# Retention and a feed-forward block on one core: written order on all engines, turns of q and k by DMA, one load list

## The chip, the cores and the metric

The kernel runs on one core of one Trainium2 chip. The metric is the device time of one execution in microseconds (us), given as the median of several. All medians, ratios and profiles below are of undisturbed ("fast") runs, except where one run is called slow. A ratio is the mean time of one kernel's fast runs over the mean of the other kernel's fast runs of the same rounds on the same chip, so it is not quite the ratio of the medians that are quoted. Intervals are 95%.

TensorE (PE in the profile) does the matrix products, VectorE (DVE), ScalarE (ACT) and GpSimd (POOL) the rest, and SyncE (SP) issues the transfers. SPq is its transfer queue.

## The reference

```python
# q, k, v: (8 batches, 8 heads, 576 tokens, 64), f32
scores = scale * q @ k.T                       # per batch and head
Dmat   = where(i >= j, gamma[h] ** (i - j), 0) # causal decay
x      = ((scores * Dmat) @ v)                 # then to (4608 tokens, 512)
out    = gelu_tanh(x @ w_in) @ w_out           # w_in 512x2048, w_out 2048x512
```

A batch is 576 tokens, that is four chunks of 128 and a tail of 64. Within a chunk the retention is computed from masked scores; what earlier chunks contribute goes through a running state (k^T v, scaled and added from chunk to chunk, the "scan"). The feed-forward part runs over nine blocks of 512 tokens. Each block has an up half (64 products `hp` with w_in, then a GELU into `gT`) and a down half (64 products `op` with w_out).

## The kernel before

The retention of batch b+1 is put between the feed-forward steps of block b. q and k come in as token rows and must be turned (transposed) before the scores. TensorE does that, and VectorE copies the result out of PSUM. Only TensorE follows the written order; a scheduler orders the other engines. All transfers go through one queue. The code here is shortened.

```python
def tr_pair(b, p):                       # turn four chunks of one head pair, one copy
    for i, key in enumerate("kq"):
        for c in range(NC):
            nc.tensor.transpose(t[:, 512*i + 128*c : ...], a[key][...], ident)
    nc.vector.tensor_copy(out=s, in_=t)  # "qk"

def att_steps(b):                        # ten pieces, all four chunks in each
    return [tr_pair 0, tr_pair 1, tr_tail, scores 0-1 + states + scan,
            tr_pair 2, tr_pair 3, scores 2 + tail, values 0-1, scores 3, values 2-3]

slots = {1: 0, 2: 1, 3: 2, 5: 3, 7: 4, 8: 5, 11: 6, 14: 7, 16: 8, 19: 9}
with tc.manual_schedule(engines={PE}):
    load_batch(0); cast_batch(0, ...)
    for g in range(4): load_w_in(g)
    load_batch(1)
    ...                                  # retention of batch 0, casts of w_in
    for f in range(NF): load_w_out(f)
    for f in range(NF): cast_w_out(f)
    for t in range(NTB):                 # feed-forward block t, with the pieces in its slots
        ...
```

Of the kernel before, what the change touches and what calls it, by code (L numbers as in the profile page):

```python
# [19 lines left out]
def kernel(  # L20
# [9 lines left out]







# [9 lines left out]
    NF = DF // 128  # L46
    scale = 1.0 / math.sqrt(D)
# [4 lines left out]
    ps = ctx.enter_context(tc.tile_pool(name="ps", bufs=2, space=PSUM))  # L52

    def bank(tag, bufs, name, dt=F32):
        return ps.tile([128, 512 if dt == F32 else 1024], dt, tag=tag, name=name, bufs=bufs)


    ident = const.tile([128, 128], F16, name="ident")
    make_identity(nc, ident)

    pos_i = const.tile([128, 1], I32, name="pos_i")
    nc.gpsimd.iota(pos_i, pattern=[[0, 1]], base=-64, channel_multiplier=1)
    pos = const.tile([128, 1], F32, name="pos")
    nc.vector.tensor_copy(out=pos, in_=pos_i)
    post = const.tile([128, 1], F32, name="post")
    nc.vector.tensor_copy(out=post[0:64], in_=pos[0:64])
    nc.vector.tensor_scalar(out=post[64:128], in0=pos[64:128], scalar1=-64.0, scalar2=None, op0=ALU.add)
    ex = const.tile([128, 24], F32, name="ex")
    for h in range(H):
        lg = math.log(gam[h])  # L70
        nc.vector.tensor_scalar(out=ex[:, h : h + 1], in0=pos, scalar1=lg, scalar2=None, op0=ALU.mult)
        nc.vector.tensor_scalar(out=ex[:, 8 + h : 9 + h], in0=pos, scalar1=-lg, scalar2=None, op0=ALU.mult)
        u, hh = divmod(h, 4)
        pr = slice(64 * u, 64 * u + 64)
        nc.vector.tensor_scalar(out=ex[pr, 16 + hh : 17 + hh], in0=post[pr], scalar1=lg, scalar2=None, op0=ALU.mult)
        nc.vector.tensor_scalar(out=ex[pr, 20 + hh : 21 + hh], in0=post[pr], scalar1=-lg, scalar2=None, op0=ALU.mult)
# [3 lines left out]
    nc.vector.tensor_scalar(out=sc[:, 16:20], in0=sc[:, 16:20], scalar1=scale, scalar2=None, op0=ALU.mult)  # L80

    gt = const.tile([128, HP, 64], F32, name="gt")
    for h in range(H):
        u = 64 * (h % 2)
        nc.gpsimd.memset(gt[u : u + 64, h // 2, :], gam[h] ** 128)

    cm = const.tile([128, NC, 128], F32, name="cm")
    nc.gpsimd.memset(cm, 1.0)
    nc.gpsimd.affine_select(
        out=cm, in_=cm, compare_op=ALU.is_ge, fill=0.0, base=0,  # L90
        pattern=[[0, NC], [1, 128]], channel_multiplier=-1,
    )
    tm = const.tile([128, 2, 128], F32, name="tm")
    nc.gpsimd.tensor_copy(out=tm, in_=cm[:, 0:2, :])
    nc.gpsimd.memset(tm[0:64, :, 64:128], 0.0)

    tbd = []
    for i in range(2):
        t = const.tile([128, NC, HP, 128], F16, name=f"tbd{i}")
        nc.gpsimd.memset(t, 0.0)  # L100
        tbd.append(t)

    w_in_sb = const.tile([128, 4, DF], F16, name="w_in_sb")
    w_out_sb = const.tile([128, NF, DM], F16, name="w_out_sb")
    xT = const.tile([128, HP, NT], F16, name="xT")


    def ld():
        return sb.tile([128, 512], F32, tag="ld", name="ld", bufs=15)

    att = {}

    def load_batch(b):
        att[b] = a = {"raw": {}}
        for c in range(NC):
            for key, src in (("k", k), ("q", q), ("v", v)):
                t = ld()
                nc.sync.dma_start(  # L118
                    out=t.rearrange("p (h d) -> p h d", d=D),
                    in_=src[b, :, 128 * c : 128 * c + 128, :].rearrange("h s d -> s h d"),  # L120
                )
                a["raw"][key, c] = t
        for key, src in (("k", k), ("q", q), ("v", v)):
            t = ld()
            for u in range(2):
                nc.sync.dma_start(
                    out=t[64 * u : 64 * u + 64, 0:256].rearrange("p (h d) -> p h d", d=D),
                    in_=src[b, 4 * u : 4 * u + 4, M0:S, :].rearrange("h s d -> s h d"),
                )
            a["raw"][key, NC] = t  # L130

    def cast_batch(b, eng):
        a = att[b]
        for key in "kqv":
            a[key] = sb.tile([128, NC * 512 + 256], F16, tag="c" + key, name="c" + key, bufs=2)
        for c in range(NC + 1):
            for key in "kqv":
                w = 512 if c < NC else 256
                raw = a["raw"][key, c][:, 0:w]
                dst = a[key][:, 512 * c : 512 * c + w]  # L140
                if key == "v":
                    eng[key].tensor_copy(out=dst, in_=raw)  # L142
                else:
                    s0 = {"q": 0, "k": 8}[key] if c < NC else {"q": 16, "k": 20}[key]
                    nh = w // D
                    eng[key].tensor_tensor(  # L146
                        out=dst.rearrange("p (h d) -> p h d", d=D),
                        in0=raw.rearrange("p (h d) -> p h d", d=D),
                        in1=sc[:, s0 : s0 + nh].unsqueeze(2).to_broadcast([128, nh, D]),
                        op=ALU.mult,  # L150
                    )
        del a["raw"]

    w_raw = {}

    def load_w_in(g):
        for ct in range(4):
            t = ld()
            nc.sync.dma_start(out=t, in_=moe_w_in[128 * ct : 128 * ct + 128, 512 * g : 512 * g + 512])
            w_raw["i", g, ct] = t  # L160

    def load_w_out(f):
        t = ld()
        nc.sync.dma_start(out=t, in_=moe_w_out[128 * f : 128 * f + 128, :])
        w_raw["o", f] = t

    def cast_w(n, dst, src):
        if n % 2 == 0:
            nc.vector.tensor_copy(out=dst, in_=src)
        else:  # L170
            nc.scalar.copy(out=dst, in_=src)  # L171

    def cast_w_in(g):
        for ct in range(4):
            cast_w(ct, w_in_sb[:, ct, 512 * g : 512 * g + 512], w_raw.pop(("i", g, ct)))

    def cast_w_out(f):
        cast_w(f, w_out_sb[:, f, :], w_raw.pop(("o", f)))

# [4 lines left out]
    def tr_pair(b, p):  # L184
        a = att[b]
        t = bank("att", 6, "tr", F16)
        for i, key in enumerate("kq"):
            for c in range(NC):
                nc.tensor.transpose(  # L189
                    t[:, 512 * i + 128 * c : 512 * i + 128 * c + 128],  # L190
                    a[key][:, 512 * c + 128 * p : 512 * c + 128 * p + 128],
                    ident,
                )
        s = sb.tile([128, 1024], F16, tag="qk", name="qk", bufs=6)
        nc.vector.tensor_copy(out=s, in_=t)  # L195
        a["qk", p] = s

    def tr_tail(b):
        a = att[b]
        t = bank("att", 6, "tr", F16)  # L200
        for i, key in enumerate("kq"):
            for s in range(2):
                nc.tensor.transpose(
                    t[:, 256 * i + 128 * s : 256 * i + 128 * s + 128],
                    a[key][:, 512 * NC + 128 * s : 512 * NC + 128 * s + 128],
                    ident,
                )
        s = sb.tile([128, 512], F16, tag="qkt", name="qkt", bufs=2)
        nc.vector.tensor_copy(out=s, in_=t[:, 0:512])
        a["qkt"] = s  # L210

    def score_pairs(b, pairs, tail):
        a = att[b]
        todo = []
        for p in pairs:
            st = [bank("att", 6, "st") for _ in range(2)]
            qk = a["qk", p]
            for c in range(NC):
                for hl in range(2):
                    r = slice(64 * hl, 64 * hl + 64)  # L220
                    nc.tensor.matmul(  # L221
                        st[hl][:, 128 * c : 128 * c + 128],
                        qk[r, 128 * c : 128 * c + 128],
                        qk[r, 512 + 128 * c : 512 + 128 * c + 128],
                        start=True, stop=True,
                    )
            for hl in range(2):
                todo.append((("ret", p, hl), st[hl], 512))
        if tail:
            st = [bank("att", 6, "st") for _ in range(2)]  # L230
            qk = a["qkt"]
            for s in range(2):
                for hl in range(2):
                    r = slice(64 * hl, 64 * hl + 64)
                    nc.tensor.matmul(
                        st[hl][:, 128 * s : 128 * s + 128],
                        qk[r, 128 * s : 128 * s + 128],
                        qk[r, 256 + 128 * s : 256 + 128 * s + 128],
                        start=True, stop=True,
                    )  # L240
            for hl in range(2):
                todo.append((("rett", hl), st[hl], 256))
# [145 lines left out]
    with tc.manual_schedule(engines={PE}):  # L388
        load_batch(0)
        cast_batch(0, {"k": nc.vector, "q": nc.gpsimd, "v": nc.gpsimd})  # L390
        for g in range(4):
            load_w_in(g)
# [51 lines left out]
```

## Time and profile before

Median 361.18 us (360.8 to 361.42 in three runs). The profiled span is 358.8 us.

| stretch of the trace | us |
|---|---|
| block 0 ends (start of the whole until then) | 87.06 |
| block 1 | 35.47 |
| block 2 | 35.13 |
| blocks 3 to 6 | 35.12, 35.93, 35.50, 35.50 |
| blocks 7 and 8 without retention, and the end | 59.09 |

The way to read such a kernel is to find the first `hp` of each block in TensorE's timeline and to take differences. TensorE is busy for nearly all of every block after block 0, so there its own work and its short waits set the time. In block 0 it is busy 53.21 of 87.06 us, so there something else does.

### The profile page before, as it was taken

Reading aid. Unit: us, or ns where it says so; the run is one execution under the profiler, and the core shown is the slowest. Engines: PE = TensorE matmul, PEld = TensorE weight load, DVE = VectorE, ACT = ScalarE, POOL = GpSimd, SP = SyncE. Lnnn points to the kernel's source line nnn. Section 1 sums busy time; section 2 is a strip of 40 time slices with the busy share of each in tenths; the row PEclk is TensorE's granted clock in tenths of the full one; section 3 lists DMA queues with packets and bytes.
Section 4 is the critical chain, followed back from the end, with each engine's and each line's share of the span. In section 5 each row is a group of like instructions: output and inputs, shape, how many; then the busy total and the mean of one; then the engine's idle time right before and its main releaser. Section 6 shows DMA issues by size and latency. Waiting matters only on the chain.

```text
span 358.8 us, 6008 instructions
## 1 busy us (share of the span) xinstructions
PE 316.4 (88%) x2400; PEld 159.1 (44%) x2400; DVE 125.9 (35%) x269; ACT 161.9 (45%) x303; POOL 70.3 (20%) x101
## 2 busy tenths in 40 slices
PE   0176368799999999999999999999999999999995
PEld 0153134344544454455445544554454444444442
DVE  5287238430762174227422771172117200000000
ACT  1037318722682268236723662366236624714721
POOL 8610430342051333232321232000000000000000
PEclk9995669899999999999999999999999999999999
DMA  9979989994692898598937931100110011011012
GB/s 173 205 230 319 224 193 360 219 188 134 144 218 81 194 225 163 127 235 170 194 108 187 216 82 58 58 2 2 58 60 0 2 60 58 0 60 59 0 38 79
DMA packets 122715, 46.52 MB, mean 130 GB/s; under 512 B 113984, under 2 KB 113984, under 8 KB 122688
## 3 DMA queue, kind: packets, MB, share of 16 engines
q1 hardware_dynamic: 122688, 46.15, 55.2%
q8 instruction: 18, 0.29, 0.4%
q14 instruction: 9, 0.07, 0.1%
HBM read 36.70 MB, written 9.44 MB: 129 GB/s over the span
## 4 chain that ended last, share of the span: by engine, by line
PE 67%; ACT 10%; DMA 9%; DVE 7%; SPq 4%; issue 1%; POOL 1%; DVEq 0%; ACTq 0%
PE op L369 35%; PE hp L355 24%; DVE ret L246 4%; ACT gT L361 4%; SPq L118 3%; DMA ld<-in_moe_w_out_dram 3%; DMA ld<-in_q_dram 3%; ACT tbd_128 L281 2%; ACT tbd_130 L281 2%; PE xs L290 2%; DMA ld<-in_moe_w_in_dram 2%; PE xs L308 2%; PE st L221 2%; PE tr L189 2%; DVE ws L278 1%; DMA ld<-in_v_dram 1%
## 5 line engine op out<-in xcount | busy, mean ns | idle before, releaser
L355 PE MATMUL hp<-xT,w_in_sb 128*128 128x512 f16 x576 | 141.6, 388 | 7.7 <-ACT gT L361 7.5
L369 PE MATMUL op<-w_out_sb,gT 128*128 128x512 f16 x576 | 128.1, 379 | 0.0
L361 ACT ACTIVATE gT<-hp 128x512 f16<-128x512 f32 x144 | 85.2, 598 | 58.6 <-PE hp L355 57.9
L355 PEld LDWEIGHTS <-w_in_sb 128*128 128x128 f16 x576 | 54.7, 99 | 68.8 <-issue 16.7
L369 PEld LDWEIGHTS <-gT 128*128 128x128 f16 x576 | 55.6, 98 | 65.3
L377 ACT COPY ost<-op 128x512 f32<-128x512 f32 x36 | 21.1, 586 | 100.9 <-PE op L369 66.0
L246 DVE TENSOR_TENSOR ret<-st,cm 128x512 f16<-128x512 f32 x64 | 40.7, 684 | 49.5 <-PE st L221 49.4
L146 POOL TENSOR_TENSOR ck<-ld,sc 128x512 f16<-128x512 f32 (+1 forms) x35 | 34.8, 997 | 82.2 <-DMA ld<-in_k_dram 60.9
L195 DVE COPY qk<-tr 128x1024 f16<-128x1024 f16 x32 | 21.9, 686 | 56.5 <-PE tr L189 56.5
L146 DVE TENSOR_TENSOR cq<-ld,sc 128x512 f16<-128x512 f32 (+1 forms) x35 | 22.6, 660 | 40.2 <-DMA ld<-in_q_dram 40.2
L142 POOL CAST cv<-ld 128x512 f16<-128x512 f32 (+1 forms) x40 | 23.1, 590 | 67.4 <-DMA ld<-in_v_dram 36.8
L189 PE MATMUL tr<-ident,ck 128*128 128x128 f16 x128 | 14.7, 234 | 23.5 <-DVE ck L146 15.0
L189 PEld LDWEIGHTS <-ck 128*128 128x128 f16 x128 | 10.6, 104 | 31.7 <-DVE ck L146 15.5
L325 ACT CAST xT<-xs 128x512 f16<-128x512 f32 x32 | 17.2, 589 | 5.0 <-PE xs L308 4.9
L189 PE MATMUL tr<-ident,cq 128*128 128x128 f16 x128 | 14.2, 236 | 1.2 <-POOL cq L146 1.0
L281 ACT CAST tbd_128<-ws 64x256 f16<-64x256 f32 x32 | 12.9, 403 | 3.1 <-DVE ws L278 2.6
L281 ACT CAST tbd_130<-ws 64x256 f16<-64x256 f32 x32 | 12.9, 403 | 2.4 <-DVE ws L278 2.0
L171 ACT CAST w_in_sb<-ld 128x512 f16<-128x512 f32 x8 | 5.0, 620 | 19.6 <-DMA ld<-in_moe_w_in_dram 19.5
L290 PE MATMUL xs<-ret,cv 128*64 128x128 f16 x256 | 11.3, 227 | 1.3 <-DVE ret L246 1.0
L278 DVE TENSOR_TENSOR ws<-vs,gt 128x256 f32<-128x256 f32 x24 | 11.8, 492 | 1.4
L221 PE MATMUL st<-qk 64*128 64x128 f16 x256 | 11.9, 226 | 0.3 <-DVE qk L195 0.3
L221 PEld LDWEIGHTS <-qk 64*128 64x128 f16 x256 | 7.6, 98 | 9.8 <-issue 7.4
(56 smaller groups left out, 125.7 us busy)
## 6 DMA issues: line engine op xcount, KB each, us to landing
out_dram<-ost SPq DMA_DIRECT2D x36, 256.0 KB, 2.0
ld<-in_k_dram SPq DMA_DIRECT2D x32, 256.0 KB, 4.8
ld<-in_q_dram SPq DMA_DIRECT2D x32, 256.0 KB, 4.9
ld<-in_v_dram SPq DMA_DIRECT2D x32, 256.0 KB, 4.9
ld<-in_moe_w_in_dram SPq DMA_DIRECT2D x16, 256.0 KB, 6.4
ld<-in_moe_w_out_dram SPq DMA_DIRECT2D x16, 256.0 KB, 6.0
ld<-in_k_dram SPq DMA_DIRECT2D x16, 64.0 KB, 3.3
ld<-in_q_dram SPq DMA_DIRECT2D x16, 64.0 KB, 2.6
```

The costliest lines, as they stand in the source:

```text
L142: eng[key].tensor_copy(out=dst, in_=raw)
L146: eng[key].tensor_tensor(out=dst.rearrange("p (h d) -> p h d", d=D), in0=raw.rearrange("p (h d) -> p h d", d=D), in1=sc[:, s0 : s0 + nh].u ...
L189: nc.tensor.transpose(t[:, 512 * i + 128 * c : 512 * i + 128 * c + 128], a[key][:, 512 * c + 128 * p : 512 * c + 128 * p + 128], ident,)
L195: nc.vector.tensor_copy(out=s, in_=t)
L221: nc.tensor.matmul(st[hl][:, 128 * c : 128 * c + 128], qk[r, 128 * c : 128 * c + 128], qk[r, 512 + 128 * c : 512 + 128 * c + 128], start=T ...
L246: nc.vector.tensor_tensor(out=r, in0=st[:, 0:w], in1=m.rearrange("p c i -> p (c i)"), op=ALU.mult)
L281: nc.scalar.copy(out=td[r, c, :, r], in_=w[r])
L290: nc.tensor.matmul(x[64 * hl : 64 * hl + 64, 128 * c : 128 * c + 128], a["v"][:, col(c, p, hl)], a["ret", p, hl][:, 128 * c : 128 * c + 12 ...
L355: nc.tensor.matmul(hp, w_in_sb[:, ct, 128 * fc : 128 * fc + 128], xT[:, ct, TB * t : TB * t + TB], start=(ct == 0), stop=(ct == 3),)
L361: nc.scalar.activation(out=gT[:, fc, :], in_=hp, func=AF.Gelu_apprx_tanh)
L369: nc.tensor.matmul(op[i], gT[:, f, 128 * i : 128 * i + 128], w_out_sb[:, f, :], start=(f == 0), stop=(f == NF - 1),)
L377: nc.scalar.copy(out=o, in_=op[i])
```

## The change

The change puts all engines in written order and rearranges the retention by chunk instead of by head pair. Batches 3 to 7 have their q and k turned by transfers (DMA) from SBUF to SBUF, so TensorE no longer turns and VectorE no longer copies for them. x lives in a ring of 1536 tokens. One list holds all loads in the order batch 0, w_in, w_out, batches 1 to 7; a `pump` issues the next ones as staging tiles are freed by casts. The core of it, shortened (left out are constants, one GELU issued early in the set-up, and rewritten helpers with the same arithmetic; `filler(6)` is six products of the identity whose result nobody reads):

```diff
+    NPE = 3          # batches below this are turned on TensorE
+    LD = 18          # staging tiles of the load ring
+    ctx.enter_context(tc.manual_schedule())          # all engines
+    def turn_dma(b):
+        for key in "kq":
+            nc.sync.dma_start_transpose(out=a["t" + key], in_=a[key])
...
+    seq = [("b", 0, c, key) ...] + [("i", g, ct) ...] + [("o", f) ...]
+    seq += [("b", b, c, key) for b in range(1, B) ...]
+    def cast_chunk(b, c, key, eng):
+        cast(b, c, key, eng)
+        pump(int(c < NC))                            # freed tile: next load
...
-        for s in att_steps(0):
-            s()
+    for c in CH:                                     # batch 0, chunk by chunk
+        cast_chunk(0, c, ...); turn_pe(0, c, (nc.scalar.copy, nc.scalar.copy))
+        score(0, c); state(0, c); scan(0, c, nc.scalar.copy)
+        filler(6); av(0, c); put(0, c)
...
+    for b in range(1, B):
+        g0 = {1: 2, 2: 36, 3: 50, 4: 66}.get(b, 36 + 24 * (b - 3))   # where its casts stand
+        ...
+        if b >= NPE:
+            at(..., lambda b=b: turn_dma(b))         # three steps after the last cast
+        start = {1: (8, 5), 2: (5, 4), 3: (13, 2), 4: (9, 3)}.get(b, (2, 4))
+            def sc_step(b=b, c=c):
+                if b < NPE:
+                    turn_pe(b, c, (nc.vector.tensor_copy, nc.vector.tensor_copy))
+                score(b, c); state(b, c); scan(b, c, nc.vector.tensor_copy)
...
+            for i0 in (0, 2):                        # block 0, down half
+                for f in range(NF):
+                    steps.append(lambda: ([cast_w_out(f), pump(1)] if i0 == 0 else None,
+                                          [down_mm(0, i, f) for i in (i0, i0 + 1)]))
```

## The prediction

> **What bounds the kernel now.** I read the engines' busy shares first, then the busy tenths in 40 slices, then the busy time by stretch, then the chain that ended last in order of time, and last TensorE's own timeline. The page's slices say that there are two kernels in one:
>
> ```profile
> PE   0176368799999999999999999999999999999995
> PEclk9995669899999999999999999999999999999999
> DMA  9979989994692898598937931100110011011012
> ```
>
> Each digit is 9 us. For 80 us TensorE is thinly used, its clock is at half for some 30 us and the DMA engines are full; from the ninth slice on TensorE is full and the transfers fade out. The chain, in order of time, dates the seam:
>
> ```profile
> 35.76 4.51 DMA ld<-in_q_dram
> ...
> 43.76 5.12 DMA ld<-in_v_dram
> ...
> 53.38 6.53 DMA ld<-in_moe_w_out_dram
> ...
> 87.06 1.73 PE hp L355 x8
> ...
> 122.53 1.73 PE hp L355 x8
> ...
> 299.71 13.81 PE hp L355 x64
> ```
>
> The columns are start, length, what. Up to 64 us the chain is loads and what follows them: batch 0, w_in, batch 1, w_out, in that order. Feed-forward block 0 (a block is 512 tokens) ends at 87.06, block 1 at 122.53; block 6, the last one that carries retention work, ends at 299.71. Blocks 7 and 8 are bare, and the span ends at 358.8. In a steady block TensorE is the bound: the stretch from 87.0 to 122.5 has it busy 34.64 of 35.50 us, VectorE 15.60, ScalarE 17.13, GpSimd 9.62.
>
> A bare block is 128 matmuls of 13.81 / 64 us, so 27.62 us. The rest of a steady block is retention. TensorE's timeline gives it by differences of starts:
>
> ```profile
> 88.62 0.39 PE L189 MATMUL tr<-ident,ck 128*128 128x128 f16 x4
> 88.85 0.39 PE L189 MATMUL tr<-ident,cq 128*128 128x128 f16 x4
> 89.07 1.03 PE L355 MATMUL hp<-xT,w_in_sb 128*128 128x512 f16 x4
> ```
>
> Eight turns take 89.07 - 88.62 = 0.45 us, and the matmul after them does not wait: feed-forward work stands between a turn and the scores that need its copy. Summed over the block this way: turns 4 x 0.45 + 0.23 = 2.03, scores and states 1.78, value products 2.05, so 5.86 us. Block 2 lasts 157.66 - 122.53 = 35.13; less 27.62 and 5.86, 1.65 us of stalls and switching remain.
>
> **What the Trainium skill says.** "TensorE: Matmul & The Clock Gate", Part 1, says that the array's clock is halved until about 3.4 us of sustained work, and falls back after an idle window. The trace agrees: matmuls of 512 columns that start at 35.1 come 0.43 us apart, those at 299.71 come 0.216 us apart. The specification table of that page gives VectorE, ScalarE and GpSimd a strict first-in first-out queue; the argument on order rests on it, and this trace, whose order was chosen by the scheduler, does not show it by itself. Part 4 says that a transpose on TensorE leaves its result in PSUM and needs a copy afterwards; here that is the qk copy, 32 of 686 ns. "DMA: Bandwidth & Descriptors", Latency and other measured facts, gives a DMA transpose 261 GB/s on one kernel. No transfer of this kind is in the trace before, so my time for it is an estimate.
>
> **The change, part by part.** I also compared the order of instructions of both builds.
>
> (1) *Turns by DMA, batches 3 to 7.* Removes 36 turns (2.03 us of TensorE) and their copies (4 x 0.686 + 0.425 = 3.2 us of VectorE, idle half the time, so worth nothing). TensorE is the bound in blocks 2 to 6, so the 2.03 us are all on the path. Smaller, more regular pieces with two feed-forward steps between score and value product (1.72 us, against 1.3 us for the two masked copies) should cut the 1.65 us of stalls to about 0.6. A block becomes 27.62 + 3.83 + 0.6 = 32.05 us, five of them 160.3, against 299.71 - 122.53 = 177.2 before. Worth **-16.9 us**, if the turned data is there in time.
>
> (2) *Are the transfers in time?* Each batch's k and q are 128 x 2304 x 2 B = 590 KB; at 261 GB/s an estimate of 2.3 us each, some 2 to 3 us more for landing (the median of out stores here is 2.0), so 7 to 10 us for both if issue and other loads get in the way. Both wait in the one load queue. For batch 4 they stand behind block 2's last store and its scores come at step 9 of the next block: 9 x 0.863 = 7.8 us. For 5 to 7 they stand behind the second store and have four steps of 1.73 and three of 0.86: 9.5 us. Just enough; I put in **+2.5 us** for all five.
>
> (3) *Batches 1 and 2 keep TensorE turns, but in one piece.* Turn, score and state of a chunk are now consecutive in TensorE's order, so each chunk waits in place for two copies of 0.425 us and the handover, 1.1 us. Five chunks: 5.5 us. Block 1 becomes 27.62 + 5.86 + 5.5 + 0.6 = 39.6 against 35.47, so **+4.1 us**.
>
> (4) *The start.* The load order becomes batch 0, w_in, w_out, batch 1; ahead of everything is batch 0 in chunks. In written order one chunk is a closed chain: two copies on ScalarE 1.1, scores 0.45, two masked copies 1.3, scan 0.82, two state casts 0.9, x copy 0.55, handovers: 5.3 us per chunk, slower than the 3.9 us in which a chunk lands. The first starts about 9 us, so the up products begin about 33 us (35.1 before, but then stuck behind batch 1 until 48). They no longer wait for batch 1: 16.4 us of matmuls with twelve at half clock, plus about 1.4 us three times, because ScalarE casts the next w_in group after the last GELU of the one before. Up ends about 54, against 71 before. This is where the gain ought to be. But batch 1's retention, which before was spread over both halves, now falls wholly into the down half: 13.8 + 5.9 + five chunk waits of 1.1 + about 2 us of waits for masked copies = 27, and VectorE's order puts casts of batch 1's k between w_out casts, so that down steps wait for loads that were issued after all of w_out: 4 to 6 us. That gives an end of block 0 about 86 to 90, with the clock likely to drop once. Against 87.06: **+1 us**. Most of the gain of the reordered loads is given back here.
>
> Blocks 7 and 8 and the end (59.1 us) do not change. Sum: -16.9 + 2.5 + 4.1 + 1 = -9.3, so 361.2 - 9.3 = 351.9. The positions of steps look adjusted by hand, so I lean a little to the better side: **351 us**.
>
> **The rivals.** *The start gains much.* Loads up to batch 1's tail are 15.5 MB; before, they were in by about 62 us. If the written order followed the loads, block 0 could end near 64 to 72 and the total fall to 335. For it: the DMA lines are at 9 for the first ten slices, the cause of the wait. Against it: the new in-order chain per chunk (5.3 us) and the waits in place. *The DMA turn becomes the bound.* If a pair takes 15 us and not 8, each of five blocks waits some 6 us, and 30 us more make 380, slower. For it: two transfers behind stores and loads in one queue[...]; the median k load already takes 4.8 us to land. Against it: the DMA engines were idle in the second half (shares of 0.08 in the stretches from 228.7), and the steps leave 8 to 10 us. *Nothing moves.* If the clock falls to half through block 0 (TensorE is busy under 60% there), 5 to 8 us are lost and the result is within 2%.
>
> **Range and chances.** The firm part is -16.9, with 2 to 3 us of error. The start is worth -14 to +8, the DMA waits 0 to +10. Together 339 to 361 should hold it 8 times in 10. Below 354.0 is faster by over 2%: 351 is only 3 us under, which gives 0.64; over 368.4 needs slow DMA turns throughout: 0.05.
>
> **What would show it.** In the profile after: bare blocks still 13.81 per 64 matmuls; blocks 3 to 6 about 32 us from first up matmul to the next block's first (step 1); score matmuls of batches 3 to 7 waiting for the transposed k or q by 0 to 2 us each (step 2; over 5 is the second rival); block 1 near 39.6 with five TensorE waits of about 1.1 us for VectorE copies (step 3); up products starting about 33 and block 0 ending at 86 to 90 (step 4; an end before 78 is the first rival). The prediction fails most easily in step 4, which is a long chain of short waits added by hand, and in the DMA turn, for which the trace has no duration.

## The result, and the profile after

The changed kernel takes **369.94 us** (369.5 to 372.01, five runs) against 361.18. The ratio is 1.025 [1.0218, 1.0282], so it is slower by over 2%, and outside the predicted range. The profiled span is 370.3 us.

The slices of the changed kernel, in the form in which the prediction shows those of the kernel before:

```profile
PE   0667876658889999499999999999999999999996
PEclk9999999669999999699999999999999999999999
DMA  9989959994989779986799991380073002002002
```

TensorE starts earlier (the second and third slices), but there are two dents: slices 8 and 9, and slice 17, each with a clock at six tenths. Before, all dents were in the first eight slices. The blocks, in the view of busy time by stretch (start and end, length, then busy us of each engine with its instructions in brackets, then granted clock, DMA share and GB/s), first after, then before:

```profile
0.00:95.84 95.84, 64.11 (x471) 33.09 (x472) 45.71 (x108) 35.56 (x67) 32.83 (x46) 0.93 0.97 213
135.84:176.97 41.13, 35.47 (x249) 16.44 (x248) 11.42 (x25) 14.40 (x26) 11.82 (x16) 0.92 0.90 184
176.97:210.57 33.60, 33.60 (x250) 15.47 (x248) 11.41 (x25) 14.41 (x26) 11.81 (x16) 1.00 1.08 193
```

```profile
0.00:87.06 87.06, 53.21 (x441) 28.43 (x442) 40.94 (x111) 33.88 (x64) 30.56 (x51) 0.86 0.96 231
122.53:157.66 35.13, 34.62 (x286) 17.65 (x284) 15.48 (x29) 17.24 (x33) 11.32 (x14) 1.00 0.87 175
157.66:192.78 35.12, 34.56 (x285) 17.58 (x284) 14.99 (x29) 17.32 (x33) 10.15 (x14) 1.00 0.76 168
```

The ledger, after less before: block 0 **+8.8**, block 1 (40.00 against 35.47) **+4.5**, block 2 **+6.0**, blocks 3 to 6 (4 x 33.60 = 134.40 against 142.05) **-7.65**, the rest -0.15; together +11.5, which is 370.3 - 358.8. So the steady blocks did gain. Three earlier blocks lost more. The medians differ by 8.8 us and not 11.5: the profiled execution was the slowest of the five (372.01 us). Block 0 has the same code in e3, e4 and e10 below, where TensorE's timeline has it end at 94.4 to 95.6 (95.68 here), so some of the +8.8 may belong to this one execution.

**Block 0.** The up products end at 56.1, against 71 before. Then the down half takes until 95.84. TensorE's timeline there (start, length, source line, operation; in brackets the idle time before the group and what ended it):

```profile
65.54 0.99 PE L328 MATMUL op<-w_out_sb,gT 128*128 128x512 f16 x2 [1.99 <-DVE w_out_sb L355]
...
68.30 2.72 PE L328 MATMUL op<-w_out_sb,gT 128*128 128x512 f16 x6 [1.20 <-ACT w_out_sb L355]
...
77.22 1.86 PE L328 MATMUL op<-w_out_sb,gT 128*128 128x512 f16 x4 [3.85 <-DVE w_out_sb L355]
```

Each of these down steps waited for a cast of w_out (a first one, at 57.46, waited 0.76 us). VectorE's timeline says why the last of the casts was late:

```profile
72.25 0.41 DVE L196 COPY tq<-tr 128x512 f16<-128x512 f16 x1
73.15 1.29 DVE L220 TENSOR_TENSOR ret<-st,cm 128x512 f16<-128x512 f32 x2 [0.49 <-PE st L211]
...
75.33 0.59 DVE L253 CAST tbd<-ws 64x256 f16<-64x256 f32 x2
75.94 1.23 DVE L355 CAST w_out_sb<-ld 128x512 f16<-128x512 f32 x1
```

VectorE was not overloaded (22.52 of 39.73 us in the down half). The cast simply stands behind the turn's copies, the masked copies and the scan of batch 1, all of which wait for TensorE: VectorE had been idle for 4.64 us before 71.91, until TensorE's turns were there. In written order such a chain closes in on itself. (This cast and one at 66.00 took about 1.25 us, two others 0.42; why is open.) The clock fell to half twice, from about 65.5 to 72 and from about 77 to 82, each time after such a wait. The whole down half, in the view of stretches:

```profile
56.11:95.84 39.73, 27.95 (x222) 13.90 (x221) 22.52 (x45) 8.61 (x17) 17.28 (x22) 0.83 1.04 187
```

**Block 2.** TensorE's timeline at the first scores of batch 3, the first batch that is turned by DMA:

```profile
153.58 0.61 PE L211 MATMUL st<-tq,tk 64*128 64x128 f16 x8 [5.66 <-DMA tq<-cq]
...
154.48 3.50 PE L315 MATMUL hp<-xT,w_in_sb 128*128 128x512 f16 x8
```

It waited 5.66 us for the turned q, and the next eight feed-forward products took from 154.48 to 157.91, 3.43 us where eight at the full clock take 1.73. The transfer queue's own timeline shows where the turn had been:

```profile
137.47 0.36 SPq L339 DMA_DIRECT2D out_dram<-ost  x1
...
139.11 1.89 SPq L73 DMA_DIRECT2D ld<-in_k_dram  x1
...
144.58 4.18 SPq L201 DMA_TRANSPOSE tk<-ck  x1
148.86 2.83 SPq L201 DMA_TRANSPOSE tq<-cq  x1
```

Loads were issued without a pause from 137.88 until 144.5, each taking about 1 us of the queue (the DMA share of this block is 0.90); the turn came after them. Its inputs had long been ready: GpSimd's last casts of batch 3's k and q are

```profile
110.25 0.61 POOL L171 TENSOR_TENSOR ck<-lt,sc 128x256 f16<-128x256 f32 x1
110.82 0.80 POOL L171 TENSOR_TENSOR cq<-lt,sc 128x256 f16<-128x256 f32 x1
```

so the turn was issued 33 us after them. Its q half was issued at 148.86 and landed 4.7 us later. Batches 4 to 7 show no such wait.

**Blocks 3 to 6.** TensorE is busy in 33.60 of 33.60 us. One chunk of batch 5:

```profile
217.68 0.40 PE L211 MATMUL st<-tq,tk 64*128 64x128 f16 x8
218.00 0.32 PE L233 MATMUL us<-cv,ck 128*64 128x64 f16 x8
218.25 1.90 PE L315 MATMUL hp<-xT,w_in_sb 128*128 128x512 f16 x8
220.08 0.41 PE L262 MATMUL xs<-ret,cv 128*64 128x128 f16 x8
```

By differences of starts, scores take 0.32 and states 0.25 us per chunk, and the eight `hp` take 1.83, not the 1.73 of eight unbroken ones. Summed over a block, retention products are 4.98 us, and 33.60 - 27.62 - 4.98 = 1.00 us is left for the breaks.

### The profile page after: what moved, and what is told of

Same layout as the page of the kernel before. It is cut to its first block, busy times and chain, and to the rows that moved or that the text cites. A ratio compares the mean times of both kernels' runs of the same rounds, so it can differ in the third digit from the quotient of the medians.

```text
span 370.3 us, 5675 instructions
## 1 busy us (share of the span) xinstructions
PE 325.2 (88%) x2250; PEld 154.1 (42%) x2250; DVE 121.1 (33%) x271; ACT 147.0 (40%) x259; POOL 90.6 (24%) x118
## 4 chain that ended last, share of the span: by engine, by line
PE 84%; DVE 9%; ACT 4%; issue 2%; DMA 1%; SPq 0%; DVEq 0%; ACTq 0%
PE hp L315 35%; PE op L328 34%; PE st L211 4%; PE xs L262 3%; PE tr L189 2%; PE xs L280 2%; DVE ret L220 2%; PE us L233 2%; DMA tq<-cq 1%; DVE tk L196 1%; DVE ck L171 1%; DVE ws L250 1%; DVE tq L196 1%; ACT tk L196 1%; ACT gT L321 1%
## 5 line engine op out<-in xcount | busy, mean ns | idle before, releaser
L171 POOL TENSOR_TENSOR cq<-ld,sc 128x512 f16<-128x512 f32 x32 | 33.7, 1054 | 52.0 <-DMA ld<-in_q_dram 51.5
L171 POOL TENSOR_TENSOR ck<-ld,sc 128x512 f16<-128x512 f32 x20 | 20.9, 1046 | 64.7 <-PE us L233 23.1
L211 PE MATMUL st<-tq,tk 64*128 64x128 f16 x288 | 16.2, 231 | 19.4 <-DVE tq L196 8.0
L302 ACT CAST xT<-xs 128x512 f16<-128x512 f32 (+1 forms) x33 | 18.8, 572 | 35.6 <-PE xs L280 26.9
L167 POOL CAST cv<-ld 128x512 f16<-128x512 f32 x32 | 20.8, 649 | 30.2 <-issue 17.7
L211 PEld LDWEIGHTS <-tk 64*128 64x128 f16 x288 | 9.4, 98 | 31.3 <-issue 13.2
L253 DVE CAST tbd<-ws 64x256 f16<-64x256 f32 x56 | 18.3, 328 | 1.4
L262 PEld LDWEIGHTS <-cv 128*64 128x64 f16 x288 | 10.6, 116 | 18.1 <-issue 16.9
L171 DVE TENSOR_TENSOR ck<-ld,sc 128x512 f16<-128x512 f32 x12 | 10.9, 914 | 18.5 <-DMA ld<-in_k_dram 18.4
L189 PE MATMUL tr<-ident,ck 128*128 128x128 f16 x54 | 7.0, 262 | 10.5 <-DVE ck L171 10.5
L189 PEld LDWEIGHTS <-ck 128*128 128x128 f16 x54 | 4.8, 116 | 14.6 <-DVE ck L171 11.6
```

Source lines behind the costliest of these rows:

```text
L167: eng.tensor_copy(out=dst, in_=raw)
L171: eng.tensor_tensor(out=dst.rearrange("p (h d) -> p h d", d=D), in0=raw.rearrange("p (h d) -> p h d", d=D), in1=sc[:, s0 : s0 + nh].unsque ...
L189: nc.tensor.transpose(t[:, 128 * (n * i + p) : 128 * (n * i + p) + 128], a[key][:, 512 * c + 128 * p : 512 * c + 128 * p + 128], ident,)
L211: nc.tensor.matmul(st[hl][:, 128 * p : 128 * p + 128], a["tk"][r, 4 * c + p, :], a["tq"][r, 4 * c + p, :], start=True, stop=True,)
L253: cp(out=td[r, c, :, r], in_=w[r])
L262: nc.tensor.matmul(xs[64 * hl : 64 * hl + 64, 128 * p : 128 * p + 128], a["v"][:, col(c, p, hl)], a["ret"][c, hl][:, 128 * p : 128 * p + 128],
```

## The experiments

The eighteen kernels below all gave correct results. The theory at first had three parts: w_out's casts stand behind other work (block 0), the turns in place wait (block 1), batch 3's casts come too late for its turn (block 2). The rival was that the DMA turn is a bad trade in itself. The names e1 to e19 (e15 was never submitted) are those that the recorded expectations use. The kernel that an edit starts from is named each time.

### One repair at a time: e1, e2, e3, and e4 for the DMA turn

**e1**, from the changed kernel: all of w_out is cast before the first down step.

```diff
+    for f in range(NF):
+        cast_w_out(f)
+        pump(1)
...
-                        [cast_w_out(f), pump(1)] if i0 == 0 else None,
```

> Edit: in block 0 all sixteen w_out casts are issued before the first down step, not one per step, so VectorE no longer has batch 1's k casts and masked copies ahead of them. Theory A (written order of VectorE): the TensorE waits for w_out casts of 0.76, 1.99, 1.20 and 3.85 us go, and the clock has less reason to drop; block 0 ends at 86 to 90 instead of 95.8 and the time is 361 to 364. Rival B (batch 1's loads come too late, or the half clock of 64 to 83 us is there anyway): the waits move to the turns of batch 1, the time stays 367 to 371.

Measured 367.74 us, ratio to the kernel before 1.017. In TensorE's timeline block 0 ended at 84.24 (95.68 in the changed kernel), 11.4 us earlier, so the reading of block 0 was right: its down half took 28.58 us, and the same 222 products kept TensorE busy for 23.09 us, at a clock of 1.00. But block 1 then took 47.1 us instead of 40.0. ScalarE's timeline and the transfer queue's show the new wait:

```profile
89.72 0.58 ACT L337 COPY ost<-op 128x512 f32<-128x512 f32 x1 [4.91 <-DMA out_dram<-ost]
```

```profile
88.06 2.03 SPq L73 DMA_DIRECT2D ld<-in_v_dram  x1
90.18 1.36 SPq L339 DMA_DIRECT2D out_dram<-ost  x2
```

ScalarE had no free staging tile (`ost`, three of them) because stores stood in the queue behind loads; its GELUs stood behind that copy, and TensorE waited 4.73 us for `gT`.

**e2**, from the changed kernel: for batches 1 and 2 each chunk is turned one feed-forward step before its scores.

```diff
-                if b < NPE:
-                    turn_pe(b, c, ...)
+            if b < NPE:
+                at(b - 1, u - 1, lambda b=b, c=c: turn_pe(b, c, ...))
```

> Edit: for batches 1 and 2 the turn of a chunk is written one feed-forward step ahead of its scores. Theory A: the waits of scores for the turned copies (0.85 us each in blocks 0 and 1) go; block 1 falls from 40.0 to about 36.2 us, block 0 by 2 to 4; time 363 to 366. Rival C (the excess of block 1 is the finer grouping of the small matmuls and not the wait): block 1 stays above 38.5 and the time above 368.

Measured 367.01, ratio 1.015. Block 1 fell to 37.3 us and TensorE's waits for the turn's copies from 8.0 to 2.8 us; but batch 3's turn was now awaited for 6.8 us instead of 5.66.

**e3**, from the changed kernel: batch 3's casts, and with them its turn, twelve steps earlier.

```diff
-        g0 = {1: 2, 2: 36, 3: 50, 4: 66}.get(...)
+        g0 = {1: 2, 2: 36, 3: 38, 4: 66}.get(...)
```

> Edit: casts of batch 3 written twelve steps earlier, so that its DMA turn is issued before block 1's last store and not behind it and seven loads. Theory A (late issue): the 5.66 us wait in block 2 and the half clock after it go, block 2 falls from 41.1 to about 33.8 us; time 362 to 364. Rival D (a DMA turn beside full loads is itself too slow): a wait of some us remains at the first scores of batch 3, time 366 to 370.

Measured 372.27, ratio 1.0309: a miss. No wait for the turn is seen, but only because TensorE came to it late: ScalarE waited 12.4 us for a staging tile whose store stood behind loads, and TensorE 7.7 us for `gT`. The turn itself was still issued at 140.58, though its casts had been done at 114.6 (111.6 in the changed kernel: GpSimd had run ahead of TensorE there too, so the edit moved places in the queue and not the casts). "The casts come too late" was therefore not the cause.

**e4**, from the changed kernel: every batch turned on TensorE, in place.

```diff
-    NPE = 3
+    NPE = 8
```

> Edit: the DMA turn undone alone, all batches turned on TensorE in place. Theory A: a block of 33.6 us gets 2.0 us of turns and five waits of 0.85 to 0.95 us, so about 40 us like block 1; blocks 3 to 6 +26, block 2 -1; time about 394. Rival E (the DMA turn gains nothing because the DMA engines hold up something else): time 368 to 375.

Measured 394.93, ratio 1.0923, as expected. The steady blocks took 39.93 us. The view of waits (engine, line, what it waited for: us in total, times, longest) names the cause:

```profile
PE st L211 <- DVE tq L196: 27.9, 35, 0.9
```

So the DMA turn saves 6.33 us per block against turning in this place. It is not a bad trade; that rival falls for this order of work.

### Repairs together: e5, e6, e7; and the load order alone in the kernel before: e8

**e5** is e1 with eight staging tiles, **e6** is e3 with eight, **e7** is e1, e2 and e3 together with eight.

```diff
-        o = sb.tile([128, DM], F32, tag="ost", name="ost", bufs=3)
+        o = sb.tile([128, DM], F32, tag="ost", name="ost", bufs=8)
```

> Edit: w_out casts first as in the first run, and eight output staging tiles in place of three. In the first run block 0's down half ended at 84.2, 11.6 us earlier than in the changed kernel, but 7.1 us came back in block 1: ScalarE waited 4.9 us for a staging tile whose store stood behind loads in the one queue, its GELU behind that, and TensorE's clock fell. Theory F (the stores' place in the queue): with eight tiles that wait goes, block 1 is 40 us again, time 357 to 360. Rival B: some other wait holds block 1 and the time stays 365 to 368.

> Edit: batch 3's casts and DMA turn twelve steps earlier, as in the third run, and eight staging tiles. In the third run the wait for the turn (5.66 us) was gone, but ScalarE waited 12.4 us for a staging tile and TensorE 7.7 us for its GELU. Theory F: both gone, block 2 about 34 us, time 362 to 364. Rival D: the turn is late whenever loads are in flight, time 367 or more.

> Edit: w_out casts first, turns of batches 1 and 2 one step ahead, batch 3 twelve steps earlier, eight staging tiles. Theory A with F: block 0 ends at 80 to 81, block 1 37.3, block 2 34, four blocks of 33.6, end 59.1: span 345, time 346 to 349, faster than the kernel before by 3 to 4%. If the waits only move on, 355 or more.

Measured: e5 364.54 (ratio 1.0098), e6 374.07 (1.0366), e7 363.02 (1.0056). All three missed. The wait for staging tiles was gone in each, but the wait for batch 3's turn grew to 8.4, 9.4 and 11.3 us. In e7, queue and TensorE:

```profile
133.33 2.30 SPq L339 DMA_DIRECT2D out_dram<-ost  x3
135.73 3.72 SPq L201 DMA_TRANSPOSE tk<-ck  x1
```

```profile
144.28 0.61 PE L211 MATMUL st<-tq,tk 64*128 64x128 f16 x8 [11.30 <-DMA tq<-cq]
```

Batch 3's casts had been done at 111.5 in this run, yet its turn was issued at 135.73. Between them stand 18 loads of 256 KB and the tail of one batch, issued one behind the other from 109 to 133, and a group of three stores. They were there because the early casts freed staging tiles, and each freed tile pumps a load into the list *ahead* of the turn. This gave the new theory: **the order of the one queue**. Whatever wait is removed, something else collides in that queue, as long as casts put loads ahead of the turn that the casts are for.

**e8**, from the kernel before: only the load order of the change (w_out ahead of batch 1), and batch 1's retention in the last ten steps of block 0.

```diff
-        load_batch(1)
         for s in att_steps(0):
...
             load_w_out(f)
+        load_batch(1)
...
+            if t == 0:
+                slots = {i + 14: i for i in range(10)}
```

> Edit on the kernel before: only the new load order (w_out ahead of batch 1), with batch 1's retention moved into the last ten steps of block 0, everything else as before. Theory G (the load order is worth something where order is left to the scheduler): up products of block 0 do not stall behind batch 1's turns, block 0 ends at 72 to 80 and the time is 346 to 354. Rival: the loads in sum are the bound of the start, block 0 ends at 85 or later, time 358 to 364.

Measured 359.05, ratio 0.9941 [0.992, 0.9963], nearer the rival. The up products ran unbroken from 34.91 to 50.79, but TensorE then waited 3.27 and 3.49 us for GpSimd's casts of batch 1, whose loads are now later. Block 0 ended at 82.75 instead of 86.90 (both in TensorE's timeline). The load order, with this place for batch 1, moves the loss from one place to another and keeps some 2 us.

### The queue: e9, e10, e13, e18

**e9**, from e7: loads that batch 3's casts free are held back until that batch's turn is issued, right after its last cast (three steps earlier than before, with only loads between). **e10** puts this edit alone into the changed kernel.

```diff
+    held = {}
     def cast_chunk(b, c, key, eng):
         cast(b, c, key, eng)
-        pump(int(c < NC))
+        if b == NPE == 3:
+            held[b] = held.get(b, 0) + int(c < NC)
+            if (c, key) == (NC, "v"):
+                turn_dma(b)
+                pump(held[b])
+        else:
+            pump(int(c < NC))
...
-        if b >= NPE:
+        if b > NPE:
```

> e7_three_ost8, with one thing more: the loads that batch 3's casts free are held back until the DMA turn of that batch is issued, so that in the one queue the turn no longer stands behind loads of batches 4 and 5. Theory (order of the one queue): the wait of 11.3 us for batch 3's turn and the half clock behind it go, block 2 takes 33.6 to 35 us instead of 47.1, the whole 347 to 351 us, 3% faster than the kernel before. Rival (the turn itself is slow while loads run, or another wait is behind it): block 2 stays over 40 us and the time at 356 or more.

> The changed kernel with the hold of the loads alone, batch 3 cast at its written place. Theory: the wait of 5.66 us for batch 3's turn and its half-clock products go, block 2 takes some 35 us instead of 41.1, block 0 and block 1 stay at 95.8 and 40 us, the time is 362 to 365. Rival (the casts themselves come too late, not the queue): the wait stays at 4 us or more and the time at 367 to 371.

Measured: e9 361.2 (ratio 0.9992), e10 375.46 (1.0379). By their times both missed, but the traces decide it otherwise. In both, batch 3's wait was gone and block 2 took 33.5 us. The loss had moved one block on. In e9 it is batch 4's turn, still in its old place behind loads and the stores of block 2 (queue, then TensorE):

```profile
163.10 1.12 SPq L339 DMA_DIRECT2D out_dram<-ost  x2
164.32 3.91 SPq L201 DMA_TRANSPOSE tk<-ck  x1
```

```profile
173.09 0.61 PE L211 MATMUL st<-tq,tk 64*128 64x128 f16 x8 [9.76 <-DMA tq<-cq]
```

Batch 4's casts had been done since 136.9. In e10, which has three staging tiles, it is a store behind loads, and block 3 took 46.6 us (ScalarE's timeline):

```profile
178.51 0.58 ACT L337 COPY ost<-op 128x512 f32<-128x512 f32 x1 [13.98 <-DMA out_dram<-ost]
```

**e13**, from e9: the hold for every batch that is turned by DMA. The turn of batch 4 thereby also goes ahead of one store, those of batches 5 to 7 ahead of two. **e18**, from the changed kernel: that hold and eight staging tiles, nothing else.

```diff
-        if b == NPE == 3:
+        if b >= NPE:
...
-        if b > NPE:
-            g = g0 + 17
-            at(1 + (g - 34) // 24, (g - 34) % 24, lambda b=b: turn_dma(b))
```

> e9_three_hold with the hold for batches 3 to 7: each batch's turn is issued right after its last cast, and the loads that its casts free come after it. Theory (order of the one queue): batch 4's wait of 9.8 us and the half clock behind it go, blocks 2 to 6 all take 33.6 us, the time is 349 to 352, against 361.2 of e9. Rival (the turn is slow in itself, or held loads come too late for the next batch's casts): a wait of 3 us or more stays in some block and the time at 355 or more.

> The changed kernel with the hold for batches 3 to 7 and eight staging tiles for stores, nothing else. Theory (the queue costs block 2 its 7.5 us, the start and block 1 are other causes): block 0 still ends near 95 and block 1 takes 40 us, blocks 2 to 6 take 33.6 each, the time is 361 to 364. Rival (some later batch now waits for loads or turns): a wait of 3 us or more in blocks 2 to 6 and the time at 367 or more.

Measured: e13 **349.15**, ratio 0.9657 [0.9609, 0.9705]; e18 363.73, ratio 1.0081 [1.0035, 1.0128]. Both as the theory said. In e13 no wait for a DMA turn is left, and blocks 2 and 3 take 33.53 and 33.64 us. Its slices:

```profile
PE   0577878879889999999999999999999999999995
PEclk9999999999999999999999999999999999999999
```

Both dents are gone. In e18 the queue's share (hold and staging tiles together) stands alone: 369.94 - 363.73 = 6.2 us, with block 2 at 33.5 and the waits for w_out and for turns in place still there.

### The start: e11, e14, e19

**e11**, from e9: batch 0's next chunk is cast and turned before the scores of the chunk at hand, and w_in is cast one group ahead. **e14** is the same edit on e13.

```diff
+    first(0)                       # cast and turn chunk 0
     for c in CH:
+        if c < NC:
+            first(c + 1)
         score(0, c)
...
+    w_in_group(0)
     for g in range(4):
+        if g < 3:
+            w_in_group(g + 1)      # cast group g+1 ahead of the ups of group g
```

> e9_three_hold with the start in another order: batch 0's next chunk is cast and turned before the scores of the chunk at hand, and the casts of w_in stand one group ahead of the up products. Theory (the chunk chain of 5.7 us bounds the start): the up products begin at 26 to 29 us instead of 34.7 and the time falls by 6 to 8 us against e9, to 340 to 344. Rival (loads or ScalarE's copies bound the start anyway): the up products begin after 32 us and the gain is 3 us or less.

> e13_hold_all with the start of e11_start. Theory: the start gives 3.5 to 7 us once no later wait swallows it: 343 to 348, 4% to 5% faster than the kernel before. Rival (time gained at the start brings a batch too early for its loads): no faster than e13.

Measured: e11 357.72 (ratio 0.99 [0.9863, 0.9937]), 3.5 us less than e9, between the two expectations. The run of e11 that was profiled was slow (411.81 us, clock 0.767), so nothing is read from its trace. e14 takes **343.87** us, ratio 0.9531 [0.9486, 0.9577], 5.3 us less than e13. In e14 the up products begin at 27.58 (34.85 in e13), with one wait of 0.7 us for a cast of w_in, where e13 has four with 3.6 together. That shows that the chunk chain and the place of w_in's casts, not the loads, had set the start; the two were not tried apart. The rival is true in part: the up half ends 10.9 us earlier (44.12 against 55.02), block 0 only 7.2 (74.96 against 82.19), and block 1 gives back 1.6 more (39.38 us against 37.78), where TensorE waited up to 1.98 us for a cast of batch 2's q. e14 beats both kernels.

**e19**, from e14: w_out is cast again between the down steps, as the change wrote it (the reverse of e1's edit).

> e14_hold_start with w_out cast again between the down steps of block 0, as the change wrote it. Theory (TensorE waits for casts that stand behind other work in VectorE's order, and its clock falls): block 0 ends 7 to 12 us later than e14's 74, the time is 350 to 355. Rival (with the faster start the loads of w_out bound block 0 either way): the time within 3 us of e14's 343.9.

Measured 352.73, ratio 0.976, 8.9 us more than e14, as the theory said. The view of waits shows the cost:

```profile
PE op L328 <- DVE w_out_sb L355: 10.4, 4, 4.1
```

### What the DMA turn is worth: e12, e17; and the breaks: e16

**e12**, from e7: no DMA turn, every chunk turned on TensorE one step ahead of its scores (`NPE = 8`). **e17** adds e11's start to it.

> e7_three_ost8 with all batches turned on TensorE, each chunk one step ahead of its scores, so without any DMA turn. It tells what the DMA turn is worth against a well ordered turn in place. Theory (turn ahead needs no wait for VectorE): steady blocks take 35.6 to 36.5 us, being 33.6 plus some 2 to 2.8 us of turns, the time is 357 to 363. Rival (VectorE bounds the turn's copies even so): steady blocks stay at 39 us or more and the time at 375 or more.

> e12_three_pe with the start of e11_start: no DMA turn, every chunk turned on TensorE one step ahead of its scores, loads in their first order. Theory: e12's 360.7 less what the start gives (3.5 to 7 us), 354 to 357, so that the DMA turn's worth against e14 is five times 2.2 us, about 11. Rival: the start gains nothing here, 360 to 361.

Measured: e12 360.71 (ratio 0.998 [0.9936, 1.0024]), e17 355.68 (0.9862 [0.9812, 0.9911]), both as the theory said. TensorE's timeline of e12 shows why the wait for the copies is gone:

```profile
165.67 1.03 PE L315 MATMUL hp<-xT,w_in_sb 128*128 128x512 f16 x4
166.68 0.40 PE L211 MATMUL st<-tq,tk 64*128 64x128 f16 x8
```

One feed-forward step between turn and scores hides VectorE's copies. A steady block takes 35.83 us, so the DMA turn is worth some 2.2 us per block against a well-placed turn on TensorE (33.60 in the changed kernel, 33.67 on average in e13), not the 6.33 of e4. Five blocks give about 11 us; e12 less e13 is 11.6, e17 less e14 is 11.8.

**e16**, from e13: a chunk's value products at the step of the next chunk's scores, so that TensorE leaves the feed-forward products less often.

```diff
-            at(b - 1, u + 2, lambda ...: (av(b, c), put(b, c)))
+            at(b - 1, u + (4 if b >= NPE and c < NC else 2), lambda ...)
```

> e13_hold_all with the value products of a chunk put at the step of the next chunk's scores, so that each of batches 3 to 7 leaves the feed-forward products four times less. Theory (about 0.1 us at each return to full-array products): steady blocks take 33.2 us instead of 33.6, the whole some 2 us less than e13. Rival (the return costs nothing, the small products themselves are longer than counted): blocks stay at 33.6 and the time within 0.5 us of e13.

Measured 349.2 against e13's 349.15, and block 2 took 33.54 against 33.53: the rival's time. TensorE's timeline of e16:

```profile
232.63 0.41 PE L262 MATMUL xs<-ret,cv 128*64 128x128 f16 x8
232.98 0.40 PE L280 MATMUL xs<-tq,tbd 128*128 128x128 f16 x4
233.31 0.40 PE L211 MATMUL st<-tq,tk 64*128 64x128 f16 x8
```

Here the four products L280 last 0.33 us from start to start; in e13, where an `hp` follows them, 0.23. Sixteen unbroken `hp` take 3.55 us where two groups of eight took 3.66. What was saved on `hp` is paid on L280. That fits a fee of about 0.1 us wherever products on half the array (64 rows or columns) follow products on all of it; e16 moved those places and hardly cut their number. This reading is argued from the timelines, not tested by a run that cuts their number.

## Why the prediction was wrong, point by point

**Step 4, the start, was the largest error.** It predicted +1 us; the trace shows +8.8. Its parts held up to the end of the up half: the first up product at 34.7 (33 predicted) and the end at 56.1 (54). What failed is the sum of the down half: 39.7 us, where the prediction had 27 and 4 to 6 for w_out's casts. Term by term, waits for turns in place were 4.0 us (5.5 predicted), waits for w_out's casts 7.8 (4 to 6), and, the larger term, TensorE was busy for 27.95 us with work that was put at 19.7. In e1 the same 222 products take 23.09 us at the full clock, so, as an estimate, 4.9 us are the half clock and 3.4 us products that are longer in the finer form. The prediction said that the clock would "likely drop once" and named no time for it (its terms sum to 85 to 87, so its 86 to 90 leaves 1 to 3 us); it dropped twice.

The reason for the waits was half right: the prediction had down steps wait for late loads of batch 1. VectorE did wait for such a load, once (4.51 us before 57.30), but the longest wait, 3.85 us, was for a cast that stood behind batch 1's copies and scan. e1 and e19 show that the place of the casts is the cause: with w_out cast ahead, block 0 ended 11.4 us earlier, and undoing that in the best kernel cost 8.9.

**Step 2, transfers in time, was right in size and wrong in place.** Both turns together took 9.0 us from the first issue to the last landing in block 2; 7 to 10 was the estimate. But the step counted what stands ahead of a turn only for batches 4 to 7, where there was no wait at all, and overlooked batch 3, which falls where loads still flood the queue. There the cost was 41.13 - 33.60 = 7.5 us, against 2.5 for all five. e9, e10 and e13 show that it is the queue's order: the hold takes the wait away, while writing the casts earlier (e3, e6, e7) made it longer or put a wait for stores in front of it. No run gave the turns or the stores a queue of their own. The rival "the DMA turn becomes the bound" was right only in its form, a wait over 5 us, and only for one batch.

**Step 1, turns by DMA, was right in mechanism and mis-sized in one term.** The turns left TensorE and the stalls vanished, but a block became 33.60 us, not 32.05. The term 3.83 + 0.6 for retention and stalls (redone on block 2 of the trace before, scores and states are 2.02 and not 1.78, so 4.07 + 0.6) measured 5.98: 4.98 for the same products in smaller groups, 1.00 for the breaks. For five blocks that is 7.75 us less gain. e12 shows why the step's arithmetic missed: in this finer form a turn on TensorE would cost some 2.2 us, about the 2.03 that was counted, so the turns were priced rightly and the finer chunks were not.

**Step 3, batches 1 and 2, was right for block 1, partly by luck.** Block 1, which carries batch 2, took 40.0 us (39.6 predicted). The five waits were there, but came to 4.0 us and not 5.5, while TensorE's work was 35.95 us and not 34.1: two errors that cancel. e2 shows what the waits are worth: 8.0 us fall to 2.8 over both batches, and block 1 to 37.3.

The sum of the prediction was -9.3. Replacing the terms by the measured ones gives block 0 +8.8, block 1 +4.5, block 2 33.60 + 7.53 - 35.13 = +6.0, blocks 3 to 6 -7.65: +11.6. The expected gain was not hidden behind something else in the steady blocks; it was partly never there (finer chunks) and mostly paid out again in blocks 0 and 2. (A reading to put right: TensorE's share of block 0 before was 61%, not "under 60%".)

By experiments the way from 369.9 to 343.9 divides so: the queue 6.2 us (e18); w_out's casts, the turns of batches 1 and 2 ahead of their scores and batch 3's earlier place together 14.6 (e13 less e18); the start 5.3 (e14).

## What to carry to other kernels

When all engines run in written order, look at every cast that a matrix product needs and ask which earlier instruction of the same engine waits for that same product's engine. When loads, stores and turns share a queue, decide what may stand ahead of a turn or a store; a freed buffer that issues the next load at once puts that load ahead of urgent work, and in e6 and e7 writing the casts earlier made it worse. Repairs that show no gain alone (e3, e9, e10) can each be right; the trace, not the time, tells whether the wait went away or moved.

## What the Trainium skill lacked or had wrong

- "DMA: Bandwidth & Descriptors", Latency and other measured facts, gives a DMA transpose in that section by its bandwidth alone (261 GB/s on one kernel, so my estimate of 2.3 us for 590 KB). In the changed kernel each turn held the queue for 2.7 to 4.2 us at issue and landed 4.7 to 6.7 us after its issue began; batch 3's pair took 9.0 us.
- That page gives no figure for what it costs to mix loads, stores and turns in one queue. Here a turn whose input was ready at 111.5 was issued at 135.73 (e7), and a store kept ScalarE waiting for 13.98 us (e10).
- No page gives a time for changing between products on the whole array and on half of it; it would belong in "TensorEngine Tiling (Array Packing)". The timelines here show about 0.1 us at each such change (eight `hp` in 1.83 us instead of 1.73), some 1 us per block; that the change is the cause is argued, not tested.
